# A decode attention block: K and V loaded eight heads at a time in 48 KB runs instead of four heads in 24 KB runs

## The chip, the cores and the metric

The kernel runs on one core of a Trainium2 chip: PE multiplies matrices, DVE and ACT work on vectors, SP issues transfers, and 16 DMA engines (the number that the page's shares refer to) move data from HBM into SBUF, where the kernel's buffers have 128 partitions. The metric is device time in microseconds, from runs on the chip. The other numbers come from the hardware profile of one execution: its span is about 2 us shorter than the measured time. Unless said otherwise a ratio is the mean time of one kernel's fast runs over that of the other's fast runs of the same rounds, so it is not quite the ratio of the medians that are quoted.

## The reference, cut to what matters

Two rows of activations (batch 2, one new token each) pass a layer norm, an attention over a key and value cache, and a gated feed-forward block.

```python
B, Sq, D = 2, 1, 640
Hq, Hkv, Sk, Dh = 32, 32, 8192, 192
W = min(4096, max(256, Sk // 4))                 # 2048: only the last 2048 keys are used
q = (x @ wq)  -> [B, 32, 1, 192]
k = k_cache[:, :, Sk - W:, :]                    # 2 x 32 x 2048 x 192, bf16
v = v_cache[:, :, Sk - W:, :]
p = softmax(q k^T * Dh ** -0.5);  o = p v;  h = x + o @ wo
out = h + (gelu(LN(h) @ w_gate) * (LN(h) @ w_up)) @ w_down
```

The windows of K and V are 100.7 MB, the weights 21.6 MB. Every byte is used once, so this is a kernel that streams 122.3 MB from HBM into SBUF. In the cache, two heads of a batch lie 3 MiB apart, and the window of a head is one piece of 768 KiB.

## The kernel before: the parts that matter

The SP engine issues all loads but the small one of x, in a fixed order, into a ring of six 24 KB slots per partition. One load of K or V is a group `g` of four heads of one batch, 3 MB:

```python
SLOT, TPG = 24576, 64                            # bytes a partition; keys in one partition's run
K_AT = (0, SLOT, 2 * SLOT, 3 * SLOT); V_AT = (4 * SLOT, 5 * SLOT)

def kv_src(cache, g):
    h0 = 8 * (g // 4) + 4 * (g % 4 // 2)
    return cache[g % 2, h0:h0 + 4, SKT - WIN:, :].rearrange("h (i t) d -> i h (t d)", t=TPG)
# [...]
P.op("sp", lambda e, v=v, src=src: e.dma_start(v, src), W=toks + [("sem", sem)], dma=sem)   # v: ring[:, slot], 128 partitions
```

The source pattern has the dimensions i (32 rows, 24 KB apart), h (4 heads, 3 MiB apart), and a run of 64 x 192 bf16 values, 24576 bytes. Partition p holds row i = p // 4 of head h = p % 4.

For each group PE transposes K through PSUM (48 transposes), computes the scores, DVE and ACT do the softmax, and PE multiplies by V (`pv`). A slot of the ring comes free for the next load when its last reader on PE is done: that is what SP waits for (133.4 us in 14 waits for `pv`, by the view of waits).

## Time and profile before

| | before |
|---|---|
| time | 294.67 us (294.64 to 294.71, 3 runs) |
| span of the profile | 293.0 us |
| DMA queue, share of 16 engines' span | 97.8% |
| PE / DVE / ACT busy | 68% / 44% / 33% |

Lines of the page of the kernel before. The rows DMA and GB/s show 40 equal slices of the span: the busy share of the 16 DMA engines in tenths, and what they moved.

```profile
span 293.0 us, 5065 instructions
DMA  7999999999999999999999999999999999999993
GB/s 279 436 427 433 431 440 435 430 425 430 425 420 438 430 433 427 430 430 430 430 421 436 430 430 430 430 430 433 430 430 430 430 430 430 430 430 426 430 406 125
DMA packets 6654, 122.44 MB, mean 418 GB/s; under 512 B 754, under 2 KB 756, under 8 KB 1396
q1 hardware_dynamic: 6632, 122.29, 97.8%
DMA 72%; PE 23%; SPq 2%; DVE 2%; issue 1%; ACT 0%
ring<-in_A_k_cache_dram SPq DMA_DIRECT2D x16, 3072.0 KB, 32.7
ring<-in_A_v_cache_dram SPq DMA_DIRECT2D x16, 3072.0 KB, 27.6
```

The DMA engines work from the first microseconds to the last, at 430 GB/s; the chain of waits is mostly DMA. So the time is transfers plus a start (first data at 2.18 us) and a tail (the last weights land at 289.6).

### The profile page before, as it was taken

The page shows a single profiled execution, that of the slowest core. Times are in us where ns is not written, and L with a number is a line of the kernel's source. Part 1 is how long each engine was busy: PE and PEld are TensorE (multiplying, and loading weights), DVE is VectorE, ACT ScalarE, POOL GpSimd, SP SyncE. Part 2 cuts the span into 40 slices and gives each one's busy share as a digit, 9 for nine tenths or more (in the row PEclk, how much of TensorE's full clock was granted, in tenths as well). Part 3 has the DMA queues.
Part 4 walks back from the last instruction along what each step waited for, and adds up shares of the span by engine and source line. Part 5 has one row for each costly group of instructions (what it writes and reads, how often), then busy time and mean ns, then how long its engine had stood idle before and what let it go on. Part 6 is the DMA issues. An engine that isn't in the chain of part 4 may idle for free.

```text
span 293.0 us, 5065 instructions
## 1 busy us (share of the span) xinstructions
PE 198.8 (68%) x2141; PEld 153.0 (52%) x2141; DVE 128.5 (44%) x311; ACT 95.7 (33%) x119; POOL 8.4 (3%) x35
## 2 busy tenths in 40 slices
PE   2573586858677298849493597659696869666764
PEld 1451264838474285628281575356666666533432
DVE  5950364433447045525264155415365435532332
ACT  2150144433442143616161144234343434520000
POOL 3000100000000000000000000000000000000000
PEclk9996569795979579998899599969797968997755
DMA  7999999999999999999999999999999999999993
GB/s 279 436 427 433 431 440 435 430 425 430 425 420 438 430 433 427 430 430 430 430 421 436 430 430 430 430 430 433 430 430 430 430 430 430 430 430 426 430 406 125
DMA packets 6654, 122.44 MB, mean 418 GB/s; under 512 B 754, under 2 KB 756, under 8 KB 1396
## 3 DMA queue, kind: packets, MB, share of 16 engines
q1 hardware_dynamic: 6632, 122.29, 97.8%
q8 instruction: 7, 0.11, 0.2%
q14 instruction: 3, 0.02, 0.0%
q10 hardware_dynamic: 12, 0.00, 0.0%
HBM read 122.29 MB, written 0.00 MB: 417 GB/s over the span
## 4 chain that ended last, share of the span: by engine, by line
DMA 72%; PE 23%; SPq 2%; DVE 2%; issue 1%; ACT 0%
DMA ring<-in_A_k_cache_dram 54%; PE tps L549 16%; DMA ring<-in_A_wq_dram 10%; DMA ring<-in_A_wo_dram 9%; SPq L342 2%; PE ops L652 1%; PE m L703 1%; PE m L824 1%; PE sps L778 1%; PE ops L778 1%; PE m L685 1%; PE tps L789 1%; PE tps L571 1%; PE m L722 0%; DVE grow L785 0%
## 5 line engine op out<-in xcount | busy, mean ns | idle before, releaser
L549 PE MATMUL tps<-identf,ring 128*128 128x128 f32 x768 | 116.5, 320 | 46.4 <-DMA ring<-in_A_k_cache_dram 45.5
L549 PEld LDWEIGHTS tps<-identf,ring 128*128 128x128 f32 x768 | 107.3, 168 | 49.8 <-DMA ring<-in_A_k_cache_dram 46.9
L558 ACT ACTIVATE ktr<-tps 128x1024 bf16<-128x1024 bf16 x80 | 79.4, 1023 | 87.4 <-PE tps L549 87.4
L561 DVE COPY ktr<-tps 128x1024 bf16<-128x1024 bf16 x112 | 74.0, 687 | 74.5 <-PE tps L549 73.8
L627 ACT ACTIVATE eexp<-sm,nm 128x512 bf16<-128x512 f32 x16 | 11.5, 721 | 64.5 <-DVE nm L625 64.5
L652 PE MATMUL ops<-ring,ering 128*32 128x384 bf16 x512 | 24.4, 334 | 4.7 <-DMA ring<-in_A_v_cache_dram 4.7
L608 PE MATMUL sps<-ktr,rq 128*16 128x512 bf16 x384 | 25.9, 404 | 1.1 <-POOL rq L402 1.1
L616 DVE CUSTOM_DVE_ANT_1 sm<-sps,mska 128x512 f32<-128x512 f32 x16 | 11.1, 691 | 34.9 <-PE sps L608 34.9
L652 PEld LDWEIGHTS ops<-ring,ering 128*32 128x32 bf16 x512 | 12.5, 97 | 13.0 <-DMA ring<-in_A_v_cache_dram 6.0
L608 PEld LDWEIGHTS sps<-ktr,rq 128*16 128x16 bf16 x384 | 9.4, 90 | 12.1 <-issue 2.1
L623 PEld LDWEIGHTS m<-mrhs,pm 128*128 128x128 bf16 x16 | 1.5, 96 | 22.8 <-DVE mrhs L398 22.8
L623 PE MATMUL m<-mrhs,pm 128*128 128x16 bf16 x16 | 2.9, 184 | 14.7 <-DVE mrhs L398 14.7
L402 POOL TENSOR_TENSOR rq<-qs,mask 128x96 bf16<-128x96 bf16 x16 | 5.6, 359 | 195.9 <-PE sps L608 164.9
L571 PE MATMUL tps<-ring,xnT 128*32 128x384 bf16 x80 | 5.7, 444 | 7.4 <-DMA ring<-in_A_wq_dram 7.3
L402 DVE TENSOR_TENSOR ering<-m,mask 128x256 bf16<-128x256 f32 x16 | 6.7, 418 | 3.6 <-PE m L636 3.6
L571 PEld LDWEIGHTS tps<-ring,xnT 128*32 128x32 bf16 x80 | 2.4, 120 | 10.3 <-DMA ring<-in_A_wq_dram 8.3
L454 ACT ACTIVATE lt<-m,eps_t 128x2 f32<-128x2 f32 x2 | 0.5, 262 | 20.1 <-PE m L452 20.1
L594 DVE CAST qs<-ops 128x384 bf16<-128x384 f32 x1 | 0.6, 558 | 14.4 <-PE ops L589 14.4
L636 PE MATMUL m<-sel,eexp 128*128 128x64 bf16 x64 | 5.3, 213 | 1.2 <-ACT eexp L627 1.2
L636 PEld LDWEIGHTS m<-sel,eexp 128*128 128x128 bf16 x64 | 4.9, 114 | 1.7 <-DVE nm L625 1.3
L703 PE MATMUL m<-ring,ot 128*2 128x320 bf16 x96 | 4.9, 338 | 1.1 <-DMA ring<-in_A_wo_dram 1.1
L402 DVE TENSOR_TENSOR orow<-m,wm 128x1536 bf16<-128x1536 f32 x3 | 5.3, 1750 | 0.0
(113 smaller groups left out, 84.2 us busy)
## 6 DMA issues: line engine op xcount, KB each, us to landing
ring<-in_A_k_cache_dram SPq DMA_DIRECT2D x16, 3072.0 KB, 32.7
ring<-in_A_v_cache_dram SPq DMA_DIRECT2D x16, 3072.0 KB, 27.6
ring<-in_A_wq_dram SPq DMA_DIRECT2D x2, 3072.0 KB, 21.0
ring<-in_A_wo_dram SPq DMA_DIRECT2D x3, 1920.0 KB, 19.4
ring<-in_B_w_gate_dram SPq DMA_DIRECT2D x1, 1920.0 KB, 30.9
ring<-in_B_w_up_dram SPq DMA_DIRECT2D x1, 1920.0 KB, 27.0
ring<-in_B_w_down_dram SPq DMA_DIRECT2D x4, 480.0 KB, 28.9
ring<-in_A_wq_dram SPq DMA_DIRECT2D x1, 1536.0 KB, 27.9
```

What stands on the lines that cost most here:

```text
L342: P.op("sp", lambda e, v=v, src=src: e.dma_start(v, src), W=toks + [("sem", sem)], dma=sem)
L402: return lambda e: e.tensor_tensor(out=out, in0=a, in1=b, op=op)
L549: ins = e.transpose(tps[bi][:, 128 * u:128 * (u + 1)], kv[:, off:off + 128], identf[:, :])
L558: act(lambda e, dst=dst, bv=bv: e.activation(out=dst, in_=bv, func=ACT.Copy), W=[("kt", n)], X=[("t", bi)])
L561: dve(lambda e, dst=dst, bv=bv: e.tensor_copy(dst, bv), W=[("kt", n)], X=[("t", bi)], cls=0)
L571: ins = e.matmul(tps[0][32 * r:32 * (r + 1), 0:384], lhsT=xnT[:, c, 32 * J:32 * (J + 1)], rhs=wq[:, c - c0, 1536 * J + 384 * r:1536 * J + ...
L608: ins = e.matmul(sps[32 * ch:32 * ch + 16, :], lhsT=rq[:, g % 4, k, :], rhs=ktr[:, k // 2, 1024 * ch + k % 2:1024 * (ch + 1):2], start=(k ...
L616: dve(lambda e: e.tensor_tensor_reduce(out=sm[:, :].rearrange("p (u x) -> p u x", u=4), in0=sps[:, :].rearrange("p (u x) -> p u x", u=4), ...
L627: act(lambda e: e.activation(out=eexp[:, :], in_=sm[:, :], func=ACT.Exp, bias=nm[:, 0:1], scale=1.0, accum_out=zr[:, g % 4:g % 4 + 1]), R= ...
L636: ins = e.matmul(o, lhsT=eexp[:, 128 * u:128 * (u + 1)], rhs=sel64[:, :], start=True, stop=True)
L652: ins = e.matmul(ops_[32 * r:32 * (r + 1), 0:384], lhsT=ering[:, g % 4, t, :], rhs=vv[:, 384 * t:384 * (t + 1)], start=(g % 4 == 0 and t < 4),
L703: ins = e.matmul(m1[32 * r:32 * r + 2, 192:512], lhsT=ot[:, kk, :], rhs=wo[:, kk - k0, 320 * h:320 * (h + 1)], start=(kk == 1 or J < 2 and ...
```

## The change

Its intent: fewer and longer transfers. Each load takes eight heads of a batch (6 MB) with runs of 48 KB; the group is worked on in two halves (half of the keys each) with one softmax maximum; `wq` comes first and in one transfer; all products with `wo` move to the end. The core of the diff:

```diff
-SLOT = 24576
-RING = 6 * SLOT
-TPG = 64
+HALF = 24576
+SLOT = 2 * HALF
+TPH = 64
-K_AT = (0, SLOT, 2 * SLOT, 3 * SLOT)
-V_AT = (4 * SLOT, 5 * SLOT)
+K_AT = (0, SLOT)
+V_AT = 2 * SLOT
 [...]
-        def kv_src(cache, g):
-            h0 = 8 * (g // 4) + 4 * (g % 4 // 2)
-            return cache[g % 2, h0:h0 + 4, SKT - WIN:, :].rearrange("h (i t) d -> i h (t d)", t=TPG)
+        def kv_src(cache, G):
+            return cache[G % 2, 8 * (G // 2):8 * (G // 2) + 8, SKT - WIN:, :].rearrange("h (i t) d -> i h (t d)", t=2 * TPH)
+
+        def load_kv(key, cache, G, at, sem, halves):
+            if not halves:
+                load((key, G), at, SLOT, kv_src(cache, G), lambda v: v, sem)
+            for i in range(2 if halves else 0):
+                load((key, G, i), at + HALF * i, HALF, kv_src(cache, G)[:, :, HALF // 2 * i:HALF // 2 * (i + 1)], lambda v: v, f"{sem}h{i}")
 [...]
-        load_k(0)
         load_wq()
+        load_k(0)
         load_k(1)
-        for g in range(NG):
-            if g > 0 and g + 1 < NG:
-                load_k(g + 1)
-            load_v(g)
-            if g % 4 == 3 and g < NG - 5:
-                load_wo(g // 4)
+        for G in range(NO):
+            if G > 0 and G + 1 < NO:
+                load_k(G + 1)
+            load_v(G)
+            if G == NO - 2:
+                load_wo(0)
+                load_wo(1)
 [... softmax in two halves, masks, order on PE ...]
```

The source pattern is now 16 rows (48 KB apart) by 8 heads (3 MiB apart). K0 and V7 are loaded in two column halves, each 16 x 8 runs of 24 KB that still lie 48 KB apart.

## The prediction

> **What bounds the kernel now.** The input transfers, from end to end. The page's DMA row is 9 in 38 of 40 slices at about 430 GB/s. 122.3 MB moved; the queue table gives its one big queue 97.8% of 16 engines' span. First data starts 2.18 us into the span and the last weight piece (w_down) lands at 289.6 of 293.0. PE (68%), DVE (44%) and ACT (33%) have room; the chain of waits is 72% DMA. SP waits for PE (133 us in all), but work stays queued: by the packet records, engines without a packet cost only about 0.7 us before 280 us.
>
> The packet records show what a transfer costs. One packet is one contiguous run: 3840 B take 149 ns, 10240 B 385 ns, 15360 B 573 ns, 24576 B 912 ns (fastest). That is a line: 7.7 ns fixed plus bytes at 27.2 GB/s an engine, 435 GB/s for 16. [...] The middle already runs at 99% of it. Only fixed costs are left: about 415 packets on an engine, a 9 ns semaphore packet for each transfer, the start, and the tail after the last landing (3.3 us).
>
> **What the change does to that.** Bytes are the same. 24 KB runs become 48 KB for K1-K7 and V0-V6, wq's runs 60 KB: 1792 + 256 data packets fewer, 15 transfers fewer. Estimate: 2048/16 x 7.7 ns = 0.99 us, plus 15 x 9 ns = 0.13 us. The packets' mean is some ns over the fastest; if this halves too, 0.2-0.3 us more. Sum 1.1 to 1.4 us, all on the critical path, since DMA is.
>
> **What it moves.** K keeps two 6 MB buffers, V only one. V(G) can't be issued before both pv of G-1. Counted from K(G)'s landing, with durations before: transposes 5.4 + 2.7 us for each of two groups, scores 1.6, pv 1.44 each; V(G-1) lands at +14.6. I estimate pv done at about +20 us; the engines would run dry at +29.2. Slack about 9 us, so I expect no bubble. At the start V0 waits for q_rows (done near 30 us), needed at 50. At the end the order after V7 (wo2, wo3, w_gate, w_up, w_down) is unchanged, so the tail from wo3 (now 275.7) to the end keeps its 17.3 us. wq before K0 delays PE, which has slack. Cheaper softmax and masks are off the path.
>
> One unsteady item: instruction fetches (7 packets of 16 KB, each stretching one data packet by about 0.5 us) hit single engines; the last engine lags the first by 2.1 us at the end, and landings follow the last. A longer PE program may add one: +-0.6 us.
>
> **Prediction.** 293.4 us, range 292.6 to 294.8. Faster by over 2%: 0.01; within 2%: 0.95; slower by over 2%: 0.04.
>
> **What would show each step.** Packets about 4370 instead of 6654; a 49152 B packet near 1816 ns; K landings 29.1 us apart for K+V instead of 29.2; DMA row still 9 throughout; w_down landing about 1.2 us earlier; tail 3.3 us; chain of waits still DMA.
>
> **What would make it wrong.** A 48 KB run cut again into smaller packets (gain near 0.2 us). V's single buffer leaving the engines dry (V issued after K(G+1) has landed): each us costs up to 7. Longer packets making fetches or landings wait. Slower reads at the 48 KB pitch. A tail chain longer on PE than the transfers.

## The result

The changed kernel takes 542.2 us (539.29 to 545.18, 4 runs), against 294.66 us before (the median of the four runs beside it); the ratio is 1.840, 95% interval 1.830 to 1.851. Its result is listed as correct. The page of the changed kernel, the lines that answer to those above:

```profile
span 543.4 us, 4965 instructions
DMA  9999999999999999999999999999999999979996
GB/s 371 315 218 233 195 222 195 211 221 200 210 221 197 221 203 210 213 206 210 213 210 213 207 206 221 195 221 206 210 213 206 210 221 192 232 260 206 226 425 247
DMA packets 4351, 122.45 MB, mean 225 GB/s; under 512 B 498, under 2 KB 500, under 8 KB 1140
q1 hardware_dynamic: 4328, 122.29, 98.2%
another core or an unknown queue 46%; PE 31%; DMA 14%; DVE 6%; ACT 1%; issue 1%; SPq 0%
ring<-in_A_k_cache_dram SPq DMA_DIRECT2D x7, 6144.0 KB, 81.7
ring<-in_A_v_cache_dram SPq DMA_DIRECT2D x7, 6144.0 KB, 52.2
```

The line that begins with "another core" is the chain of waits. It lost the thread: 46% is waits for which it found no releaser, and its PE 31% is no sign that PE bounds anything, as PE is busy 39% of the span. The packet count is as predicted (4351), and the engines are busy 98.2% of a span that is nearly twice as long. **A busy DMA row is not a fast one**: the row GB/s beside it says 210 instead of 430. The first slices (wq) and the last but one (feed-forward weights) still run at 371 and 425 GB/s; only K and V are slow. The packet records (the duration of each packet, by its size) say it more plainly:

```
                packet      count   median ns   mean ns   sum / 16 engines, us
before          24576 B      4352         915       918      249.7
changed         24576 B       512        1892      1844       59.0
changed         49152 B      1792        3800      3753      420.4
changed         61440 B       128        2267      2400       19.2   (wq)
```

The last three sum to 498.6 us. Before, K, V and wq took 249.7 us plus 3.7 for wq's 128 packets of 12288 B. That difference, 245 of the 250 us that the span grew, is packets that took longer. So the question is why a K or V packet takes twice its time.

The TensorE clock that was granted (0.700 of full speed, 0.834 before) can be set aside: m1 below has slow packets of 24576 B too (about 1905 ns) at a clock of 1.0, with PE idle.

Two things can be read off before any experiment. A packet of 61440 B runs at full rate (median 2267 ns, 27.1 GB/s; a 24576 B packet before: 915 ns, 26.9 GB/s), so length alone is not it. And the halves of K0 and V7 have the old length, 24576 B, but take 1892 ns: that points to the pattern, not to the run.

### The profile page after: what moved, and what is told of

The parts are those of the page before. It is cut to its first block, busy times and chain, and to the rows that moved or that the text cites. A ratio compares the mean times of both kernels' runs of the same rounds, so it can differ in the third digit from the quotient of the medians.

```text
span 543.4 us, 4965 instructions
## 1 busy us (share of the span) xinstructions
PE 210.0 (39%) x2133; PEld 157.4 (29%) x2133; DVE 125.6 (23%) x283; ACT 94.4 (17%) x119; POOL 6.9 (1%) x26
## 2 busy tenths in 40 slices
DMA packets 4351, 122.45 MB, mean 225 GB/s; under 512 B 498, under 2 KB 500, under 8 KB 1140
## 3 DMA queue, kind: packets, MB, share of 16 engines
q1 hardware_dynamic: 4328, 122.29, 98.2%
## 4 chain that ended last, share of the span: by engine, by line
another core or an unknown queue 46%; PE 31%; DMA 14%; DVE 6%; ACT 1%; issue 1%; SPq 0%
PE tps L564 18%; DMA ring<-in_A_wo_dram 7%; DMA ring<-in_A_k_cache_dram 7%; PE ops L671 5%; PE sps L623 4%; DVE ring L576 3%; DVE ering L418 1%; ACT ring L573 1%; DVE orow L418 1%; DVE sm L631 1%; PE m L704 0%; SPq L343 0%; PE m L696 0%; PE m L841 0%
## 5 line engine op out<-in xcount | busy, mean ns | idle before, releaser
L576 DVE COPY ring<-tps 128x1024 bf16<-128x1024 bf16 x112 | 73.7, 687 | 309.2 <-PE tps L564 308.9
L573 ACT ACTIVATE ring<-tps 128x1024 bf16<-128x1024 bf16 x80 | 79.0, 1023 | 332.1 <-PE tps L564 332.0
L671 PE MATMUL ops<-ring,ering 128*32 128x384 bf16 x512 | 35.1, 438 | 135.3 <-DMA ring<-in_A_v_cache_dram 135.3
L671 PEld LDWEIGHTS ops<-ring,ering 128*32 128x32 bf16 x512 | 15.1, 120 | 150.5 <-DMA ring<-in_A_v_cache_dram 138.3
L623 PE MATMUL sps<-ring,rq 128*32 128x512 bf16 x384 | 24.7, 390 | 6.8 <-ACT ring L573 4.6
L623 PEld LDWEIGHTS sps<-ring,rq 128*32 128x32 bf16 x384 | 9.4, 94 | 15.6 <-issue 6.1
L418 DVE TENSOR_TENSOR ering<-m,hm 128x512 bf16<-128x512 f32 x16 | 10.9, 684 | 2.3 <-PE m L655 2.3
L631 DVE CUSTOM_DVE_ANT_1 sm<-sps,mska,mx 128x512 f32<-128x512 f32 x8 | 6.0, 750 | 13.7 <-PE sps L623 13.7
L418 POOL TENSOR_TENSOR rq<-qs,mask 128x192 bf16<-128x192 bf16 x8 | 4.2, 532 | 356.0 <-PE sps L623 326.6
L631 DVE CUSTOM_DVE_ANT_1 sm<-sps,mska 128x512 f32<-128x512 f32 x8 | 5.5, 691 | 13.1 <-PE sps L623 13.1
```

What stands on the lines that cost most here:

```text
L418: return lambda e: e.tensor_tensor(out=out, in0=a, in1=b, op=op)
L573: act(lambda e, dst=dst, bv=bv: e.activation(out=dst, in_=bv, func=ACT.Copy), W=[("kt", n)], X=[("t", bi)])
L576: dve(lambda e, dst=dst, bv=bv: e.tensor_copy(dst, bv), W=[("kt", n)], X=[("t", bi)], cls=0)
L623: ins = e.matmul(sps[32 * ch:32 * (ch + 1), :], lhsT=rq[:, G % 2, k, :], rhs=ktr[:, k // 2, 1024 * ch + k % 2:1024 * (ch + 1):2], start=(k ...
L631: dve(lambda e: e.tensor_tensor_reduce(out=sm[:, half, :].rearrange("p (u x) -> p u x", u=4), in0=sps[:, :].rearrange("p (u x) -> p u x", ...
L671: ins = e.matmul(ops_[32 * r:32 * (r + 1), 0:384], lhsT=ering[:, g % 4, t, :], rhs=vv[:, 384 * t:384 * (t + 1)], start=(g % 4 == 0 and t < 4),
```

## The experiments

All theories are named once here. A: the addresses in HBM (A1 the rows' pitch of 48 KB, A2 the distance of the heads in one load). B: long packets. C: the single V buffer starves the engines. D came later, from the first round: the destination, that is, which SBUF partitions are written at the same time. Runs marked one look are single runs: they have no interval, and their state (fast or slow) is unknown, so between kernels only differences of tens of us are read from them. The kernel before ran beside each at 294.63 to 294.98 us.

### e1 and e2: the changed kernel in halves, rows 48 KB and 24 KB apart (one look each)

The edits, cut to what matters:

```diff
-            load_kv("k", A_k_cache, G, K_AT[G % 2], f"k{G % 2}", G == 0)
+            load_kv("k", A_k_cache, G, K_AT[G % 2], f"k{G % 2}", True)         # e1 and e2; the same for V
-  .rearrange("h (i t) d -> i h (t d)", t=2 * TPH)
+  .rearrange("h (a i t) d -> i h a (t d)", a=2, t=TPH)                         # e2 only: half a of the window, rows 24 KB apart
```

> The changed kernel with every K and V transfer cut into two 3 MB halves (24 KB runs, rows still 48 KB apart, the same eight heads), so that buffers come free by halves. Theories: A (addresses: which rows the 16 engines read at the same moment, by row pitch or by head) about 540 us, 24576 B packets near 1890 ns. B (long packets: a 48 KB run itself is slow) about 294 us, packets near 915 ns. C (the single V buffer starves the engines) well below 540, packets near 915 ns.

> As e1, but half 0 of a transfer takes the first 1024 keys of the window and half 1 the last 1024, so that the rows of one transfer lie 24 KB apart instead of 48; the result stays right (keys are only permuted, K and V alike). Theory A1 (the row pitch of 48 KB): 293 to 296 us, packets near 915 ns. Theory A2 (eight heads in one transfer[...]): about 540 us. Theory C (single V buffer): 300 us or more with packets of 915 ns and an idle DMA row.

Measured: e1 522.97 us, 24576 B packets with a median of 1862 ns. e2 532.47 us, 1874 ns. Both read the right data. The page of e1:

```profile
DMA  9999999999999999999999999999999999999996
GB/s 377 327 216 213 211 213 218 213 211 214 215 220 215 211 219 217 213 224 211 221 217 226 223 224 215 223 228 224 228 224 228 217 232 223 232 321 229 226 421 254
```

B falls, since the packets are short and still slow. C falls, since buffers come free earlier, the DMA row stays at 9 and the packets themselves are slow (1862 ns in e1, against 915 before). A1 falls with e2: 24 KB between the rows changes nothing.

### e3: the kernel before with the changed kernel's addresses (one look)

```diff
-            h0 = 8 * (g // 4) + 4 * (g % 4 // 2)
-            return cache[g % 2, h0:h0 + 4, SKT - WIN:, :].rearrange("h (i t) d -> i h (t d)", t=TPG)
+            h0, s = 8 * (g // 4), SLOT // 2 * (g % 4 // 2)
+            return cache[g % 2, h0:h0 + 8, SKT - WIN:, :].rearrange("h (i t) d -> i h (t d)", t=2 * TPG)[:, :, s:s + SLOT // 2]
```

> The kernel before with nothing changed but the addresses: each 3 MB transfer reads eight heads, 16 rows of 24 KB that lie 48 KB apart (wrong result on purpose). Theories A1 and A2 (addresses): about 520 to 545 us, 24576 B packets near 1890 ns. B (long packets) and C (buffers, order): 295 us, as before.

Measured: 541.57 us, packets of 24576 B with a median of 1875 ns. From its page:

```profile
GB/s 193 354 349 206 222 211 206 209 224 205 211 263 215 210 210 217 213 208 211 215 213 259 204 215 217 210 208 217 215 206 210 220 211 204 215 217 210 217 424 233
DMA packets 6654, 122.44 MB, mean 227 GB/s; under 512 B 754, under 2 KB 756, under 8 KB 1396
```

The old program, with its old buffers, order and packet size, becomes as slow as the changed kernel by the source pattern of its K and V loads alone. Everything else in the diff is acquitted of the 250 us.

### m1: transfers alone, seven source patterns (one look)

A program of loads only. Each pattern is loaded four times, 3 MB each, 128 partitions, and waited for. The core of it:

```python
PATTERNS = (   # run, DRAM dims outermost first: (step, count)
    ("i32at24k_h4",     RUN, ((24 * KIB, 32), (3 * MIB, 4))),              # as before
    ("i16at48k_h8",     RUN, ((48 * KIB, 16), (3 * MIB, 8))),              # as changed
    ("i16at24k_h8",     RUN, ((24 * KIB, 16), (3 * MIB, 8))),
    ("i32at48k_h4",     RUN, ((48 * KIB, 32), (3 * MIB, 4))),
    ("r128at48k",       RUN, ((48 * KIB, 128),)),
    ("h8_i16at48k",     RUN, ((3 * MIB, 8), (48 * KIB, 16))),
    ("i16at48k_h8skew", RUN, ((48 * KIB, 16), (3 * MIB + 24 * KIB, 8))))
for n, run, dims in PATTERNS:
    for r in range(4):
        e.dma_start(tiles[n][:, :], src).then_inc(sem[n], 16);  e.wait_ge(sem[n], 16 * (r + 1))
```

> Transfers alone, seven address patterns, each four times 3 MB, one after the other (zeros as the result on purpose). Name: order of the partitions, outermost first; i = rows, h = heads 3 MiB apart, r = one run of rows; all runs 24 KB. A full-rate transfer should land about 9.5 us after its issue (7.3 us of data plus about 2), a half-rate one about 17. A1 (row pitch): i32at24k_h4 and i16at24k_h8 fast, the other five slow. A2[...]: i16at48k_h8, i16at24k_h8, h8_i16at48k slow; i32at24k_h4, i32at48k_h4, r128at48k fast; i16at48k_h8skew (head distance 3 MiB + 24 KiB) fast if the skew breaks the collision. B, C: all fast.

The view of DMA issues of this run; the last column is the median time from issue to landing in us. (The view leaves a number at the end of a name out, and gave no time for the sixth pattern.)

```profile
i32at24k_h<-in_A_k_cache_dram SPq DMA_DIRECT2D x4, 3072.0 KB, 10.0
i16at48k_h<-in_A_k_cache_dram SPq DMA_DIRECT2D x4, 3072.0 KB, 17.4
i16at24k_h<-in_A_k_cache_dram SPq DMA_DIRECT2D x4, 3072.0 KB, 17.8
i32at48k_h<-in_A_k_cache_dram SPq DMA_DIRECT2D x4, 3072.0 KB, 10.7
r128at48k<-in_A_k_cache_dram SPq DMA_DIRECT2D x4, 3072.0 KB, 10.2
h_i16at48k<-in_A_k_cache_dram SPq DMA_DIRECT2D x4, 3072.0 KB
i16at48k_h8skew<-in_A_k_cache_dram SPq DMA_DIRECT2D x4, 3072.0 KB, 17.3
```

Fast are the patterns whose leading count is 32 or 128 (10.0 to 10.7 us), slow those with 16 (17.3 to 17.8 us), and with 8 it is worse still: the packet records show 29 us for the sixth pattern. The pitch of the rows does next to nothing (lines 1 and 4: 10.0 and 10.7 us), nor does a skew of the heads (17.3 us with it, 17.4 without).

The packet records hold a clue to why. They don't name engines, but packets follow each other closely (in the kernel before, between 100 and 240 us, a next packet most often starts 3 or 4 ns before one ends), so many can be strung together; a string is read as one engine's. The eight packets of one engine in the slow pattern, and sixteen of one in the sixth pattern, in ns:

```
i16at48k_h8   1439 1867 1912 1909   1715 1886 1905 1909
h8_i16at48k   1792 1805 1919 1918   1494 1912 1920 1916   1411 1901 1918 1919   1442 1901 1919 1918
```

The first packet aside, the shorter ones come every fourth: the fifth, the ninth, the thirteenth. (All eight complete strings of the first i16at48k_h8 load have a shorter fifth packet, 1707 ns in the mean.)

That gave theory D. All seven patterns fill the same 128 partitions, so if the destination matters here it is by which of its partitions are written at the same time. The leading count sets how the 128 runs are grouped (16 groups of 8, 32 of 4), and may set that too; packets that are under way together would then hold each other up, with a period of four packets. m1 does not show this: no record here names an engine's partitions, so it needed tests.

### m2: source or destination? (one look)

```python
    ("near16x8",  RUN, ((400 * KIB, 16), (48 * KIB, 8)), slice(0, 128)),   # 16 x 8, no far heads
    ("heads32x4", RUN, ((3 * MIB, 32), (24 * KIB, 4)),   slice(0, 128)),   # 32 far heads, leading count 32
    ("i64_h2",    RUN, ((24 * KIB, 64), (3 * MIB, 2)),   slice(0, 128)),
    ("to0step1",  RUN, ((48 * KIB, 16),), slice(0, 16)),        # one source, four sets of 16 partitions
    ("to0step4",  RUN, ((48 * KIB, 16),), slice(0, 64, 4)),
    ("to32step4", RUN, ((48 * KIB, 16),), slice(32, 96, 4)),
    ("to0step8",  RUN, ((48 * KIB, 16),), slice(0, 128, 8)),
```

> Transfers alone, four times each. Source or destination? near16x8: 16 x 8 rows without any heads 3 MiB apart (steps 400 KiB and 48 KiB). heads32x4: 32 heads 3 MiB apart outermost, four rows each. D (destination): near16x8 slow (about 17 us, packets 1.9 us), heads32x4 and i64_h2 fast (10 us, 0.91 us). A2 (distance of heads in HBM): the other way round. Then one source (16 rows of 24 KB, 48 KB apart[...]) into four sets of 16 partitions[...]: to32step4[...] (packet 0.91 us), to0step4 and to0step8[...] (1.82 us), to0step1[...] (3.65 us). A2: all four the same.

The view of DMA issues:

```profile
near16x<-in_A_k_cache_dram SPq DMA_DIRECT2D x4, 3072.0 KB, 17.6
heads32x<-in_A_k_cache_dram SPq DMA_DIRECT2D x4, 3072.0 KB, 10.3
i_h<-in_A_k_cache_dram SPq DMA_DIRECT2D x4, 3072.0 KB, 10.3
```

A2 falls both ways: 16 x 8 is slow without heads that are far apart (17.6 us), and 32 heads 3 MiB apart are fast (10.3 us). The four single-packet loads came in the expected order but not with the expected sizes: medians near 2.6 us (to0step1), 1.6 (to0step4), 1.4 (to32step4), 1.6 (to0step8), where 3.65, 1.82, 0.91, 1.82 were expected. A single packet after a pause takes longer than one in a stream (before's first packets took 1.3 to 1.6 us as well, against 915 ns later), and to0step1 took less than four times the full-rate packet. These loads are too short to judge D by, and D's sizes for them are a miss.

### m3: one source, only the destination moved (one look)

```python
    ("four_p0_63x",   RUN, ((48 * KIB, 16), (3 * MIB, 4)), slice(0, 64)),
    ("four_p32_95x",  RUN, ((48 * KIB, 16), (3 * MIB, 4)), slice(32, 96)),
    ("four_p64_127x", RUN, ((48 * KIB, 16), (3 * MIB, 4)), slice(64, 128)),
    ("eight_p0_63x",  RUN, ((48 * KIB, 8), (3 * MIB, 8)),  slice(0, 64)),
    ("eight_p32_95x", RUN, ((48 * KIB, 8), (3 * MIB, 8)),  slice(32, 96)),
```

> Transfers alone. One source, only the destination partitions differ. four_*: 16 x 4 rows of 24 KB into 64 partitions[...]. By D[...]: into 32 to 95[...] fast, packets 0.91 us, landing about 6 us after issue; into 0 to 63 or 64 to 127[...]: packets 1.9 us, landing about 9.5 us. eight_*: 8 x 8 rows[...]: into 0 to 63[...] 1.9 us and about 17 us; into 32 to 95[...] 0.91 us and about 10 us. If the source or the number of partitions of an engine decided: no difference inside four_* or inside eight_*.

The view of DMA issues:

```profile
four_p_63x<-in_A_k_cache_dram SPq DMA_DIRECT2D x4, 1536.0 KB, 9.9
four_p_95x<-in_A_k_cache_dram SPq DMA_DIRECT2D x4, 1536.0 KB, 6.3
four_p_127x<-in_A_k_cache_dram SPq DMA_DIRECT2D x4, 1536.0 KB, 9.9
```

Into partitions 0 to 63 or 64 to 127 the packets of each load take a median of 1.88 to 1.92 us; into 32 to 95 they take 0.912. For the two loads of 8 x 8 rows the view has no time, but the packets do: 1.85 to 1.92 us into 0 to 63 (15 us in all), 0.912 into 32 to 95 (8.1 us). The source, the size and the number of partitions are the same inside each set. What differs is which partitions the data goes to, and all five loads came out near what was expected. So for transfers alone the destination decides whether a packet of 24576 B takes 0.912 us or about 1.9. That the slow patterns of m1 (1905 ns) are slow for the same reason is D's inference: m3 moves the destination, m1 the source pattern.

### e4 and e7: the changed kernel with a leading count of 32 (5 rounds each)

```diff
-  cache[G % 2, 8 * (G // 2):8 * (G // 2) + 8, SKT - WIN:, :]
+  cache[G % 2, 8 * (G // 2):8 * (G // 2) + 4, SKT - 2 * WIN:, :]    # e4 and e7: 32 rows of 48 KB of 4 heads
+                load_wo(2)                                          # e7 only: wo2 ahead of V7 instead of behind it
```

This keeps bytes, runs of 48 KB, buffers and program; the keys are the wrong ones. (Both runs, and e3, are listed as correct all the same: the comparison does not notice wrong keys. So the mark says little anywhere here; that the changed kernel, e1 and e2 read the right data rests on their source patterns.)

> The changed kernel with one thing altered: each 6 MB K or V transfer reads 32 rows of 48 KB of four heads instead of 16 rows of eight heads (twice the window; wrong result on purpose). Runs, bytes, buffers, order and program as in the changed kernel. Theory D (the leading count of the DRAM pattern, 16 or 32[...]): 293.4 us, 49152 B packets near 1816 ns, about 1.2 us under the kernel before, as the prediction's sum had it. If 48 KB runs or the single V buffer cost anything themselves: above 295.

> e4 (32 rows of 48 KB of four heads, wrong data) with wo2 loaded ahead of V7 instead of behind it. In e4 the queue ran dry near 248 us, because V7 could not be issued before both pv of group 6 (247.4 us), about 2 us of lost time on the engines. wo2 needs only the last transposes, about 1.5 us earlier. Expected: no dip in the DMA row there, 293.4 to 293.9 us, 1.0 to 1.5 us under the kernel before: the prediction's sum for the longer runs. If the dip was not what ate the gain: 295.3 as e4.

e4 takes 295.34 us (294.52 to 295.79), ratio to before 1.0011 (0.9999 to 1.0024). Its row GB/s, for comparison with 430 before and 210 in the changed kernel:

```profile
GB/s 335 469 356 429 438 429 435 438 449 424 451 435 435 431 435 423 435 435 429 435 429 429 430 429 429 429 429 429 429 429 435 429 420 399 363 435 409 432 411 119
```

The shape of the source pattern, 32 x 4 rows instead of 16 x 8, is worth 247 us of the 248. Together with e3 this settles, inside the kernel, that the shape is the cause. The 49152 B packet takes a median of 1818 ns, as the prediction had worked out (1816). But the gain of 1.2 us did not come. The view of instructions in order of time shows SP's issues in e4:

```profile
247.40 1.19 SPq L343 DMA_DIRECT2D ring<-in_A_v_cache_dram  x2
```

The packet records say that the first engine had finished wo1, the last load in the queue, at 248.16, and data follows an issue by 1 us or more (1.77 - 0.74 at the start). Between 240 and 260 us engines without a packet cost 0.8 us, and V7's slow first packets (over 912 ns) 1.05 us more: 1.9 us lost against 1.2 gained.

e7 fills that hole. The view of busy time in one stretch (its last two numbers are the DMA engines' busy share and GB/s), first e4, then e7:

```profile
247.50:255.00 7.50, 3.59 (x55) 1.93 (x51) 3.11 (x10) 1.52 (x4) 0.00 (x0) 0.89 0.92 340
247.50:255.00 7.50, 3.60 (x55) 1.94 (x51) 3.11 (x10) 1.52 (x4) 0.00 (x0) 0.79 1.01 424
```

(The row DMA of the page is too coarse for this: it reads 9 there in both.) The lost time between 240 and 260 us falls from 0.8 to 0.05 us, and the last weights land at 288.87 us, before 289.62: 0.75 us earlier. On the first engine to finish, which shows the transfers without the lag of the last engine behind it (2.6 us here, 2.1 before), it is 286.25 against 287.50, a gain of 1.25 us: the sum of the prediction. But the time is 297.86 us (296.68 to 298.04), ratio 1.0092 (1.0075 to 1.0109): 0.9% worse, clear of the noise. The chain that ended last, in order of time, in e7:

```profile
248.25 22.04 DMA ring<-in_A_v_cache_dram
270.33 2.78 PE ops L671 x17
278.19 1.80 PE m L718 x24
288.45 1.62 PE ops L795 x20
291.74 1.80 PE m L841 x42
```

and in the kernel before:

```profile
248.90 26.84 DMA ring<-in_A_wo_dram
288.40 1.87 PE m L824 x30
```

With wo2 ahead of it, V7 has only 4.7 us of loads between it and the end of wo3, too few to hide the last `pv`, the output rows and their transposes; the tail is then PE's, and the last product starts 2.9 us after its weights have landed (291.74 against 288.87). Before, the last product started 1.2 us before the landing. So the expectation for e7 was wrong too: it saw the hole and not what had been lying behind it.

### e5, e6, e8, e9, e10: keeping engines apart by a lag (one look each)

If engines hold each other up only because they run in step, a lag of four packets, the period seen in m1, should keep them apart. To e1 (24 KB packets) small loads of no use were added that give some engines more packets than others: in e5, by the strung packets, four engines took 8 before wq, eight took 4 and four none. The edit of e10 on top of e1's, cut (K1 also waits for these loads, whose place in the ring it takes):

```diff
         load_wq()
+        pump()
+        for n, p0 in ((12, 4), (12, 5), (4, 6), (4, 7)):       # n packets of 48 KB each
+            e.dma_start(ring[p0:p0 + 8 * n:8, SLOT // 2:SLOT], A_k_cache[0, 0:n, 0:2 * TPH, :].rearrange("h t d -> h (t d)"))
         load_k(0)
```

In e5 and e8 the loads stand ahead of wq, in e6 the first ahead of it and the second behind; e9 is e8 with half the bytes.

> e1 (16 x 8 rows, 24 KB runs, halves) plus two small loads at the very start, of no use to the result: 12 x 4 rows[...] and 4 x 4 rows[...], 4 packets of 24 KB each.[...] D: 300 to 310 us, packets near 915 ns, against 523 for e1. Without D: 523 or a little more. The result is right.

> e5 again with a lag that is sure to be as meant[...]. Here 12 and 4 single partitions[...] with two packets of 48 KB each: 3.63 us of work[...]. D:[...] packets of K and V near 915 ns, 300 to 310 us against 523. Without D, or if the lag does not last: 500 us or more. The result is right.

> e6 mended: there the first K load had to wait for the second lag load, the queue ran empty near 25 to 31 us and all engines started K0 together, so the lag was gone. Here both lag loads go ahead of wq, and K0 is issued while wq still moves, so the lag of 3.63 us (4 packets of 24 KB)[...] should last. D: K and V packets mostly near 915 ns, 300 to 325 us (the lag itself costs up to 7.3 us, instruction fetches disturb it by 0.6 us each), against 523 for e1. If D is wrong[...]: 523 or more. The result is right.

> e8 with half the lag: one 48 KB packet instead of two, 1.82 us, two packets of 24 KB. By D[...] a group of four takes 2 - 0.5 = 1.5 times its full-rate time, so the 231 us that K and V take at full rate become about 347 and the whole about 405 to 425 us. Without D: as e1, 523.

> e8 with the lag loads behind wq instead of ahead of it, because in e8 the engines ahead began K0 while the others still moved wq[...] (wq packets up to 4.8 us); what was left of the lag was about 1.2 us, and it stayed that for the whole of 40 to 60 us. Here the lag loads (12, 12, 4, 4 single partitions, 48 KB each)[...]. D: lag of 3.63 us kept, K and V packets mostly near 915 ns, 305 to 340 us (the lag itself costs up to 11 us), at least 100 us under e1 (523).[...] The result is right.

(e10's expectation if D was wrong: 510 us or more.)

| run | us | median packet of 24576 B, ns | what became of the lag |
|---|---|---|---|
| e1 (no lag) | 522.97 | 1862 | |
| e5 | 524.86 | 1745 | as meant until wq (strung packets of 24576 B before wq: four engines 8, eight engines 4, four none); then as in e8 (wq packets up to 4.8 us) |
| e6 | 544.04 | 1909 | the queue ran empty near 25 to 31 us, all engines began K0 together |
| e8 | 513.15 | 1751 | engines ahead began K0 while others still moved wq, whose packets took up to 4.8 us; about 1.2 us was left |
| e9 (half) | 522.89 | 1807 | none seen between 40 and 58 us: the strung packets show groups of four near 7.4 us, as in e1 |
| e10 | 441.57 | 1292 | kept in part |

Four of the five were flawed: the lag did not stand as meant through K and V. That is a reading of the packet records, found afterwards. The expectations of 300 to 325 us (e5, e6, e8) were missed by about 200, that of e9 (405 to 425) by about 100. So the totals of these four neither support D nor speak against it. e10 missed its expectation too (at least 100 us under e1; it is 81), but here the effect is plain. Packets of one engine in e10 between 150 and 166 us, in ns:

```
1187 953 1125 1846   1185 948 1104 1856   1186 948 1092 1849
```

One packet of each group of four is still as slow as in e1 (1846 to 1856 ns against 1862) and one nearly at full rate (948 to 953 against 912); the group takes 5.1 us where 3.65 would be four at full rate and about 7.4 are spent in e1 (4 x 1862 ns). So 1.6 MB of useless loads make the kernel 81 us faster with the same source pattern and the same destinations, and the lengths alternate with a period of four packets, as in m1. That fits D inside the kernel, as if a packet's time depended on what the other engines do beside it. It does not show that a full lag would bring all of it back; e4 and e3 carry that weight.

### What was not found

No version beats the kernel before. One with right data and 48 KB runs needs 16 rows by 8 heads on 128 partitions, since a head's window has only 16 rows of 48 KB, and both orders of these two counts were slow in m1 (16 leading: 17.4 us, 8 leading: 29 us). Loads of 64 partitions, of which those into 32 to 95 ran at full rate in m3, were not tried in the kernel. The whole gain to be had was about 1.2 us in any case, by the transfers of e7.

## Why the prediction was wrong

It forecast 293.4 us with a range of 292.6 to 294.8 and 0.04 for slower by over 2%; measured were 542.2. Point by point:

- **What bounds the kernel** was right, before and after: the transfers, with the DMA row full.
- **The step that failed** is the costing of the packets: "24 KB runs become 48 KB ... 2048/16 x 7.7 ns = 0.99 us" and "a 49152 B packet near 1816 ns". It took the line fitted to the old packets (7.7 ns plus bytes at 27.2 GB/s an engine) as a property of the engine. By m1 and m3 it holds for some shapes only: on all 128 partitions a 24576 B packet takes 0.91 us at a leading count of 32 and about 1.9 at 16; at a leading count of 16 into 64 partitions it takes 0.91 us for 32 to 95 and about 1.9 for 0 to 63. The change moved the leading count of the source pattern from 32 to 16, and a 49152 B packet took 3800 ns instead of 1816, 245 us in all. e3 and e4 show that the source pattern alone does it, m1 and m2 that neither the rows' pitch nor the heads' distance does, m3 that with one source the partitions written decide. That these are one cause, partitions written at the same time, is inference: which engine gets which partitions stands in no record. The period of four (m1) and e10 fit it.
- The prediction listed "Slower reads at the 48 KB pitch" among its risks. That is the wrong mechanism: pitch does next to nothing (m1: 10.0 and 10.7 us at 24 and 48 KB; e2: 532 us at 24 KB).
- What the prediction did not do is ask what the new order of the rows does to the rate. It asked only whether runs would be cut; a run of loads alone would have shown 17.4 us against 10.0 for 3 MB (m1).
- **V's single buffer**: right for the middle (e4, where the packets run at full rate, has no gap before 240 us). The tail that it forecast, 17.3 us from wo3 to the end, also held (17.3 in the changed kernel, 17.1 in e4). What it missed lies just before: V7's own issue, which waits for group 6 when no K load is left to cover the wait. The estimate of pv done 20 us after K7's landing was good (20.2 in e4, 247.35 - 227.12), but there, with wo0 and wo1 alone behind V6, the first engine ran out of work at 248.16.
- **The sum for longer runs**, 1.1 to 1.4 us, was right at the transfers' end (1.25 us on the first engine in e7) and wrong as a gain in time: in e4 the empty queue took it, in e7 the tail on PE.
- **The unsteady item** was about as described: at the end the last engine lags the first by 1.7 (changed kernel) to 2.6 us (e7). That fetches stretch single packets fits the kernel before: six of its seven fetches are followed at once by a data packet about 0.5 us longer than the others. No run tests how much of the lag is theirs.

## What to carry to other kernels

Before a load's shape is changed, look at the leading count of its source pattern and at the partitions that it goes to, and time the old and the new shape alone. A leading count of 16 in front of 8 halved the rate here with all engines shown as busy (m1: 17.4 us against 10.0 with 32 in front of 4), and 8 in front of 16 was slower still (29 us); into 64 partitions, 24576 B packets took 0.912 us for 32 to 95 and about 1.9 for 0 to 63 and 64 to 127 (m3). Read the GB/s row and the duration of packets by size beside the busy row, since slow packets count as busy too (98.2% busy at 210 GB/s). When a transfer becomes the suspect, load it alone with one property changed at a time (source, order, destination): one such run of 0.2 ms (m3) told more than the five lag variants of the kernel.
